# 86 more products on TensorE behind the last one of an attention, expert and MLP kernel

## The chip, the cores and the metric

The kernel runs on one core of a Trainium2 chip. The metric is the device time of one execution in microseconds, and all times here are microseconds unless marked ns. The engines are TensorE (PE; its loads of weights are listed as PEld), VectorE (DVE), ScalarE (ACT), GpSimd (POOL) and SyncE (SP), which issues most of the transfers.

## The reference

Three layers stand one behind the other, over 2304 tokens of width 512. Cut to what matters:

```
x = block_causal_attention(q, k, v)           # 4 x 8 heads x 576 x 64, blocks of 64
x = top-2 mixture of 8 experts(x)             # relu(x @ w1[e]) @ w2[e], weighted
h = x @ w_in                                  # 512 -> 2048
g = h * clip(h + 3, 0, 6) / 6
out = g @ w_out                               # 2048 -> 512
```

All in float32. Only the last two lines are at work where the change is made.

## The kernel before

Products are made in float32r. A value that needs more bits is split into a high and a low part (xh, xl; hh, hl; wah, wal; wbh, wbl), and three products make one: high by high, high by low, low by high.

The last layer (L1450 to L1508) works through groups of token tiles, the list GR. A tile has 128 tokens; the last groups have four tiles, 512 tokens. For each group the 2048 hidden columns are walked in 16 steps f of 128, two to a pair of weight tiles. Function m_s1 makes one step of the first product: s1 (L434) runs four parts of the inner dimension with mm3 (L428), so 12 products of 512 columns, into an accumulator named h. That tile comes from the pool ps_h, which has two buffers of one PSUM bank each. ACT and DVE read it (L1454, L1455) and make hh and hl. Function m_s2 makes the step of the second product one pair of weights later: s2 (L1089) runs three products (L1102 to L1104) for each tile into four accumulators y0 to y3, which collect over all 16 steps. With the last step the tiles are done: DVE scales tiles 0 and 2 (L1469), ACT tiles 1 and 3 (L1467), and SP sends each to the output (L1472).

The order on each engine is that in which the code is written here; an instruction waits only for the semaphores of what it reads or overwrites. Behind the last instruction the program's end (recorded under L1536) is run: SP waits for the transfers and for the engines, each engine drains, and all five meet in a barrier.

The tiles xh and xl of the last group, 128 partitions by 4 parts by 512 tokens each, are under `xT["m", len(GR) - 1]`. KD is 4, the parts of the inner dimension.

Of the kernel before, what the change touches and what calls it, by code (L numbers as in the profile page):

```python
# [7 lines left out]
F32 = mybir.dt.float32  # L8
# [144 lines left out]
def kernel(  # L153
# [1126 lines left out]
    def gather(gi, t):  # L1280
        rows = (E - 1) * CAP + EARLY * 128 if gi == 0 else E * CAP + OVF * 128
        ys = []
        for s_, w in info(gi, t):
            a = work.tile([128, DM], F32, tag="xn", name="ga", bufs=XB)
            nc.gpsimd.indirect_dma_start(  # L1285
                out=a, out_offset=None, in_=y_tab[0:rows, :],
                in_offset=bass.IndirectOffsetOnAxis(ap=s_, axis=0),
            )
            ys.append((a, w))
        gath[gi, t] = ys  # L1290
# [187 lines left out]
    for i in range(len(pairs2) + 1):  # L1478
        for r in range(2):
# [27 lines left out]
            if i < len(pairs2) and f % 2 == 0 and f // 2 < nt:  # L1507
                gather(gi + 1, f // 2)  # L1508


_INS = ["q", "k", "v", "moe_w_gate", "moe_w_noise", "moe_noise", "moe_w1", "moe_w2", "moe2_w_in", "moe2_w_out"]
_OUTS = [((2304, 512), "float32")]
# [28 lines left out]
```

## Time and profile before

| | |
|---|---|
| runs | 1084.88, 1082.29, 1084.93 |
| median | 1084.88 |
| profiled execution, its own time | 1082.07 |
| its span, first to last instruction | 1080.2 |
| granted TensorE clock, mean over the span | 0.998 of full |

The span is inside the profiled execution's time; 1.87 lie around it. In a row of a product, the time is from its start to its modelled end, and the next product starts before that end: how often TensorE can start one is read from the differences of the starts. A product's form is written as the rows and columns of its stationary operand (128*128), then the output's partitions and columns (128x512).

### The profile page before, as it was taken

The page shows a single profiled execution, that of the slowest core. Times are in us where ns is not written, and L with a number is a line of the kernel's source. Part 1 is how long each engine was busy: PE and PEld are TensorE (multiplying, and loading weights), DVE is VectorE, ACT ScalarE, POOL GpSimd, SP SyncE. Part 2 cuts the span into 40 slices and gives each one's busy share as a digit, 9 for nine tenths or more (in the row PEclk, how much of TensorE's full clock was granted, in tenths as well). Part 3 has the DMA queues.
Part 4 walks back from the last instruction along what each step waited for, and adds up shares of the span by engine and source line. Part 5 has one row for each costly group of instructions (what it writes and reads, how often), then busy time and mean ns, then how long its engine had stood idle before and what let it go on. Part 6 is the DMA issues. An engine that isn't in the chain of part 4 may idle for free. (4 is left out here: it accounts for less than half of the span.)

```text
span 1080.2 us, 17109 instructions
## 1 busy us (share of the span) xinstructions
PE 1062.4 (98%) x6189; PEld 932.8 (86%) x6189; DVE 777.3 (72%) x1471; ACT 525.8 (49%) x1061; POOL 295.7 (27%) x346
## 2 busy tenths in 40 slices
PE   7999999999999999999999999999999999999998
PEld 6999999988988989999888898988888888888886
DVE  9778787887698888897887745776655755665452
ACT  6777777754433342424233335664544545454342
POOL 6568687613110101110100001653401420410000
PEclk9999999999999999999999999999999999999999
DMA  7534432116977768766646315312202111201001
GB/s 192 143 89 128 128 89 57 23 43 213 351 250 261 278 221 295 234 214 196 215 153 218 108 35 193 97 39 59 53 26 69 40 49 40 68 10 39 1 1 39
DMA packets 120428, 133.94 MB, mean 124 GB/s; under 512 B 60693, under 2 KB 81685, under 8 KB 120341
## 3 DMA queue, kind: packets, MB, share of 16 engines
q1 hardware_dynamic: 106917, 103.32, 30.7%
q0 software_dynamic: 6080, 19.93, 6.1%
q10 hardware_dynamic: 7344, 9.57, 2.5%
q8 instruction: 50, 0.82, 0.3%
q14 instruction: 37, 0.30, 0.1%
HBM read 92.94 MB, written 36.70 MB: 120 GB/s over the span
## 5 line engine op out<-in xcount | busy, mean ns | idle before, releaser
L430 PE MATMUL h<-xh,wah 128*128 128x512 f32 (+8 forms) x832 | 275.1, 331 | 1.0 <-ACT xh L401 0.8
L431 PE MATMUL h<-xl,wah 128*128 128x512 f32 (+8 forms) x832 | 271.4, 326 | 0.4 <-DVE xl L406 0.3
L432 PE MATMUL h<-xh,wal 128*128 128x512 f32 (+8 forms) x832 | 271.4, 326 | 0.0
L1102 PE MATMUL y<-wbh,hh 128*128 128x512 f32 (+1 forms) x576 | 226.0, 392 | 2.5 <-issue 2.1
L1103 PE MATMUL y<-wbl,hh 128*128 128x512 f32 (+1 forms) x576 | 225.9, 392 | 0.1
L1104 PE MATMUL y<-wbh,hl 128*128 128x512 f32 (+1 forms) x576 | 225.5, 391 | 0.0
L430 PEld LDWEIGHTS h<-xh,wah 128*128 128x128 f32 x832 | 156.5, 188 | 14.8 <-ACT xh L401 1.0
L431 PEld LDWEIGHTS h<-xl,wah 128*128 128x128 f32 x832 | 156.6, 188 | 14.1 <-DVE xl L406 0.9
L432 PEld LDWEIGHTS h<-xh,wal 128*128 128x128 f32 x832 | 156.4, 188 | 11.4
L1104 PEld LDWEIGHTS y<-wbh,hl 128*128 128x128 f32 (+1 forms) x576 | 107.4, 186 | 25.3 <-DVE hl L457 0.8
L1102 PEld LDWEIGHTS y<-wbh,hh 128*128 128x128 f32 (+1 forms) x576 | 107.5, 187 | 23.6 <-issue 2.6
L1103 PEld LDWEIGHTS y<-wbl,hh 128*128 128x128 f32 (+1 forms) x576 | 107.4, 186 | 21.4 <-POOL wbl L385 0.8
L1455 DVE SCALAR_TENSOR_TENSOR r<-r,h 128x512 f32<-128x512 f32 (+1 forms) x80 | 50.5, 631 | 98.1 <-ACT r L1454 97.9
L453 ACT ACTIVATE hh<-h 128x288 fp32r<-128x288 f32 (+7 forms) x128 | 53.3, 416 | 130.6 <-PE h L432 98.1
L385 DVE TENSOR_TENSOR wal<-wa,wah 128x1024 fp32r<-128x1024 f32 x80 | 106.3, 1329 | 13.7 <-ACT wah L381 12.8
L385 DVE TENSOR_TENSOR wbl<-wb,wbh 128x1024 fp32r<-128x1024 f32 x76 | 102.5, 1348 | 14.7 <-ACT wbh L381 14.6
L1454 ACT ACTIVATE r<-h,three 128x512 f32<-128x512 f32 (+1 forms) x80 | 51.6, 645 | 118.7 <-PE h L432 118.7
L1075 POOL DMA_INDIRECT xn<-x_tok,sids x35 | 37.1, 1061 | 254.8 <-PE xps L398 243.4
L1458 DVE TENSOR_TENSOR hl<-r,hh 128x512 fp32r<-128x512 f32 (+1 forms) x80 | 56.0, 700 | 51.5 <-ACT hh L1457 51.5
L381 ACT CAST wbh<-wb 128x1024 fp32r<-128x1024 f32 x80 | 84.0, 1049 | 12.6 <-PE y L1104 10.5
L769 ACT ACTIVATE P<-sb,nm 128x192 f32<-128x192 f32 (+4 forms) x144 | 74.6, 528 | 29.2 <-DVE nm L763 29.2
L1457 ACT CAST hh<-r 128x512 fp32r<-128x512 f32 (+1 forms) x80 | 46.2, 577 | 86.1 <-DVE r L1455 86.1
(265 smaller groups left out, 1765.4 us busy)
## 6 DMA issues: line engine op xcount, KB each, us to landing
wa<-in_moe_w_dram SPq DMA_DIRECT2D x23, 512.0 KB, 6.2
wb<-in_moe_w_dram SPq DMA_DIRECT2D x23, 512.0 KB, 7.1
y_tab<-yo SPq DMA_DIRECT2D x32, 256.0 KB, 4.1
w<-in_moe_w_in_dram SPq DMA_DIRECT2D x16, 512.0 KB, 6.8
y_tab<-zero SPq DMA_DIRECT2D x8, 1024.0 KB, 8.1
w<-in_moe_w_out_dram SPq DMA_DIRECT2D x16, 512.0 KB, 5.3
x_tok<-x SPq DMA_DIRECT2D x32, 144.0 KB, 2.8
wa<-in_moe_w_dram ACTq DMA_DIRECT2D x9, 512.0 KB, 6.3
```

The costliest lines, as they stand in the source:

```text
L381: nc.scalar.copy(w_s[which, u][0], raws[PS[u]][which])
L385: (nc.gpsimd if e == "POOL" else nc.vector).tensor_tensor(lo, raws[PS[u]][which], hi.bitcast(F32), op=OP.subtract)
L430: nc.tensor.matmul(ps, lhsT=wh, rhs=xh, start=first, stop=False)
L431: nc.tensor.matmul(ps, lhsT=wh, rhs=xl, start=False, stop=False)
L432: nc.tensor.matmul(ps, lhsT=wl, rhs=xh, start=False, stop=last)
L453: nc.scalar.activation(h[0][:, c0:c1], ps[:, :c1 - c0], AF.Relu)
L769: nc.scalar.activation(o, views.pop((p, i)), AF.Exp, bias=nms.pop((p, i)), scale=1.0, accum_out=rs[p % 3][:, i:i + 1])
L1102: nc.tensor.matmul(yps[t][:n], lhsT=hh[:, sl], rhs=wh[:, f % 2], start=first, stop=False)
L1103: nc.tensor.matmul(yps[t][:n], lhsT=hh[:, sl], rhs=wl[:, f % 2], start=False, stop=False)
L1104: nc.tensor.matmul(yps[t][:n], lhsT=hl[:, sl], rhs=wh[:, f % 2], start=False, stop=last)
L1454: nc.scalar.activation(r[:, :n], ps[:, :n], AF.Relu, bias=three, scale=1.0)
L1458: nc.vector.tensor_tensor(hl[:, :n], r[:, :n], hh[:, :n].bitcast(F32), op=OP.subtract)
```

## The change

Behind the last loop, 86 products are written. Each has a part of xl as its stationary operand and the same part of xh as its moving operand; all start and end their accumulation in one instruction, and nobody reads the two accumulators pa and pb, which are taken from ps_h under the same tag as h. A product named full uses 128 rows of the array; low uses partitions 0 to 63 and writes pa, high uses partitions 64 to 127 and writes pb. The stationary operand has 128 columns in all of them.

```
+    xh, xl = xT["m", len(GR) - 1]
+    pa, pb = (ps_h.tile([128, 512], F32, tag="h", name="h") for _ in range(2))
+
+    def trial(n, rows, ps, k):
+        nc.tensor.matmul(ps[:, :n], lhsT=xl[rows, k % KD, 0:128], rhs=xh[rows, k % KD, :n], start=True, stop=True)
+
+    full, low, high = slice(0, 128), slice(0, 64), slice(64, 128)
+    for k in range(8):
+        trial(512, full, (pa, pb)[k % 2], k)
+    for n in (512, 384, 288, 256, 128):
+        for k in range(6):
+            trial(n, low, pa, k)
+            trial(n, high, pb, k)
+    for k in range(4):
+        trial(512, full, (pa, pb)[k % 2], k)
+        trial(512, low, pa, k)
+        trial(512, high, pb, k)
+    for k in range(6):
+        trial(256, low, pa, k)
```

So there are 8 full products of 512 columns, 6 pairs at each of five widths, 4 rounds of one full product and a pair of 512 columns, and 6 products of 256 columns on the lower half alone. The last product raises TensorE's semaphore, for which SP waits among its closing waits.

On TensorE the rows behind the last product of the fourth tile (y_11015 is the accumulator of that tile) are these, with + for what is new:

```order
 L1103 MATMUL y_11015<-wbl,hh 128x512
 L1104 MATMUL y_11015<-wbh,hl 128x512
-L1536 UNCONDITIONAL_BRANCH
+L1514 MATMUL h<-xh,xl 128x512 x20
+L1514 MATMUL h<-xh,xl 128x384 x12
+L1514 MATMUL h<-xh,xl 128x288 x12
+L1514 MATMUL h<-xh,xl 128x256 x12
+L1514 MATMUL h<-xh,xl 128x128 x12
+L1514 MATMUL h<-xh,xl 128x512 x12
+L1514 MATMUL h<-xh,xl 128x256 x6
+L1556 UNCONDITIONAL_BRANCH
```

Seven runs of products stand between the last old one and the branch to the program's end; the first 20 are the 8 full ones and the 6 pairs of 512 columns. No other engine's rows move; the branch has only another line number.

## Rows read from the trace of the kernel before

**Rows 1.** The page: busy time by engine, slices of TensorE's clock, the closing chain.
```profile
PE 1062.4 (98%) x6189; PEld 932.8 (86%) x6189; DVE 777.3 (72%) x1471; ACT 525.8 (49%) x1061; POOL 295.7 (27%) x346
...
PEclk9999999999999999999999999999999999999999
...
PE 34%; POOL 1%; DVE 1%; ACT 1%; issue 0%
```

**Rows 2.** Timeline of the end: start, length, engine, line, form, idle time before and its releaser.
```profile
1068.66 0.69 DVE L1455 SCALAR_TENSOR_TENSOR r<-r,h 128x512 f32<-128x512 f32 x1 [3.46 <-ACT r L1454]
...
1074.27 0.39 PE L1104 MATMUL y<-wbh,hl 128*128 128x512 f32 x1
...
1075.63 0.39 PE L1104 MATMUL y<-wbh,hl 128*128 128x512 f32 x1
1076.06 0.60 ACT L1467 ACTIVATE yo<-y 128x512 f32<-128x512 f32 x1 [0.76 <-PE y L1104]
1076.10 0.91 SPq L1472 DMA_DIRECT2D out_dram<-yo  x2
```

**Rows 3.** Output transfers (L1472) and program's end (L1536): ns min/median/max, first and last start.
```profile
DMA to landing us min/median/max: 2.0/2.1/2.1
...
L1536 SPq EVENT_SEMAPHORE  x9: 28/28/28, 1077.1 to 1079.1; - x9
...
L1536 SPq EVENT_SEMAPHORE  x11: 17/28/28, 1077.1 to 1080.2; - x11
...
L1536 PEldq DRAIN  x2: 13/2140/4267, 1071.8 to 1079.6; - x2
```

**Rows 4.** Last stretch: length; PE, PEld, DVE, ACT, POOL busy; granted clock; DMA share; GB/s.
```profile
1077.00:1081.00 4.00, 0.00 (x0) 0.00 (x0) 0.00 (x0) 0.00 (x0) 0.00 (x0) 0.66 0.34 130
```

**Rows 5.** Timeline of TensorE: first and last product of rows of 384, 288 and 256 columns.
```profile
612.77 0.34 PE L430 MATMUL h<-xh,wah 128*128 128x384 f32 x1
...
614.17 0.34 PE L432 MATMUL h<-xh,wal 128*128 128x384 f32 x1
...
367.62 0.30 PE L430 MATMUL h<-xh,wah 128*128 128x288 f32 x1
...
369.08 0.30 PE L432 MATMUL h<-xh,wal 128*128 128x288 f32 x1
...
235.00 0.28 PE L430 MATMUL h<-xh,wah 128*128 128x256 f32 x1
...
235.94 0.28 PE L432 MATMUL h<-xh,wal 128*128 128x256 f32 x1
```

**Rows 6.** Timeline of TensorE in the attention: narrow products, and stationary operands of 64 columns.
```profile
22.89 0.60 PE L781 MATMUL tb<-ident,P 128*128 128x128 f32 x4
...
33.68 0.28 PE L755 MATMUL sb<-kh,qd0h 128*128 128x64 f32 x1
...
33.90 0.28 PE L755 MATMUL sb<-kh,qd0l 128*128 128x64 f32 x1
...
27.52 0.25 PE L813 MATMUL tb<-pth,sp_v 128*128 128x192 f32 x1
27.61 0.28 PE L813 MATMUL tb<-ptl,sp_v 128*64 128x192 f32 x2
27.73 0.50 PE L813 MATMUL tb<-pth,sp_v 128*128 128x64 f32 x2
```

**Rows 7.** Groups of weight loads by form: busy us, mean ns of one, idle before.
```profile
L813 PEld LDWEIGHTS tb<-ptl,sp_v 128*64 128x64 f32 x96 | 11.6, 136 | 0.0
...
L1104 PEld LDWEIGHTS y<-wbh,hl 128*128 128x128 f32 x544 | 102.2, 188 | 23.2 <-DVE hl L457 0.8
```

**Rows 8.** Two stretches near the start, in the columns of rows 4.
```profile
10.00:15.00 5.00, 2.63 (x16) 1.85 (x16) 4.48 (x10) 3.15 (x9) 3.28 (x4) 1.00 0.39 71
15.00:20.00 5.00, 4.15 (x18) 3.74 (x18) 4.81 (x10) 3.32 (x8) 4.09 (x6) 0.68 0.63 134
```

## The prediction

> **What bounds the kernel now.** I read the page first, then the last microseconds as a timeline, then the program's closing rows. TensorE (PE) is busy 98% of the span at a granted clock of 9 tenths or more in all 40 slices, and the closing chain is a row of its products [rows 1]. The last three groups of instructions before the end step from product to product without a gap: L1104 starts at 1074.27 and, six products later, at 1075.63, so a product of 512 columns takes 1.36/6 = 0.227 [rows 2]. The last product starts at 1075.63 and lasts 0.39, to 1076.02. ScalarE scales that tile from 1076.06 for 0.60, and SyncE issues its last output transfer, two issues taking from 1076.10 to 1077.01 [rows 2]. A transfer lands 2.1 after its issue [rows 3], so the last one, issued at about 1076.7, lands at about 1078.8. SyncE runs through its closing waits from 1077.1 to 1079.1; 1.1 later, at 1080.2, the last barrier event ends the span [rows 3]. TensorE had reported itself drained at 1071.8 + 4.27 = 1076.07 [rows 3], and from 1077 on no engine computes at all, while the DMA engines still move the outputs [rows 4]. So TensorE bounds the kernel up to 1076.0 and the landing of the last output bounds it behind that. What is hung behind the last product has about three microseconds in which it costs nothing, from 1076.0 to 1079.0; after that each microsecond counts in full, because the barrier waits for TensorE too.
>
> **The change, part by part.** Nothing is removed or moved. 86 products are added behind the last one on TensorE, and they wait for nothing: the two accumulators come from the pool of the h tiles, whose last reader (VectorE, L1455) runs from 1068.66 for 0.69 and is done at 1069.35 [rows 2], and the operands are the last group's token tiles, in use since long before. Nobody waits for their results, so ACT, VectorE and the output transfers at 1076 to 1079 go on as before. The first added product therefore starts one step behind the last old one, at 1075.63 + 0.227 = 1075.86.
>
> What one product costs is its step, from its start to the next start, not the 0.39 of its row, since products overlap. Steps by width, all with a stationary operand of 128 columns that is loaded for each product: 512 columns 0.227 [rows 2]; 384 columns 612.77 to 614.17 in eight steps, 0.175 [rows 5]; 288 columns 367.62 to 369.08 in eleven, 0.133 [rows 5]; 256 columns 235.00 to 235.94 in eight, 0.118 [rows 5]. Below that the step stops falling: four products of 128 columns take 0.60 in all, and with 0.28 for the last one, as a product of 64 columns has it, the three steps are 0.107; products of 64 columns start at 33.68 and, two further, at 33.90, 0.11 apart [rows 6]. I take 0.109. That floor is the loading of the weights, and not the product: with a stationary operand of only 64 columns the step falls to 0.09 and 0.03, from 27.52 to 27.61 and on to 27.73 [rows 6], and the load itself is shorter, 0.136 against 0.188 [rows 7]. So: a full load occupies the loading path for 0.109, and a product occupies its part of the array for its columns.
>
> No row of this trace has a product on half of the array's rows: the stationary operand is written rows*columns, and it is 128*128 or 128*64 everywhere [rows 6, 7]. So what a pair costs has to be bounded. The upper end is one behind the other: each of a pair pays its own step. The lower end is a pair that costs what one product costs. A middle value follows from the load: the two halves stream side by side, but the two loads still come one after the other, so a pair takes the larger of one product's step and 2 x 0.109 = 0.218. That is 0.227 for 512 columns and 0.218 for 384, 288, 256 and 128.
>
> The three sums. The 8 full products take 8 x 0.227 = 1.82, and the last six, all on the lower half, 6 x 0.118 = 0.71, in every case.
> - One behind the other: five widths, 12 products each, 12 x (0.227 + 0.175 + 0.133 + 0.118 + 0.109 = 0.762) = 9.14; the four rounds of one full and two halves 12 x 0.227 = 2.72. Sum 14.39.
> - Middle: 6 x (0.227 + 4 x 0.218 = 1.099) = 6.59; four rounds 8 x 0.227 = 1.82. Sum 10.94.
> - Lower end: 6 x 0.762 = 4.57; four rounds 1.82. Sum 8.92.
>
> I take the middle. The halves have rows, weights and accumulators of their own, which speaks for products side by side. For the loads the nearest row is the floor at 64 and 128 columns: loads of 0.188 overlap in part and still come no closer than 0.109 to each other [rows 6, 7], and a load of 64 rows has as many columns as one of 128. Both ends stay in the range.
>
> In the sentences of the Trainium skill: TensorE: Matmul & The Clock Gate, LDWEIGHTS (loading the stationary operand), says that a load's time goes with the columns and not with the rows, which speaks for the middle; the estimate by that section, 128/1.2 = 107 ns, agrees with the floor of 109 above. Part 3 of that page (Packing small matmuls) has products on different row groups start some 4 ns apart, which would give the lower end where loads don't hold them up. No run here shows either for half rows yet.
>
> From the sum to the time. The last product of 256 columns starts at 1075.86 + 10.94 - 0.12 = 1086.68 and lasts 0.28 [rows 5], so TensorE ends at 1086.96. Behind it stands the closing sequence of SyncE and the barrier, which took 1.1 from the last of SyncE's waits and 1.4 from the last landing [rows 3]; I take 1.2. Span 1088.2 in place of 1080.2: 8.0 more. That is 10.94 + 0.16 (the last product's own length less its step) + 1.2, less the 4.34 that already lay between 1075.86 and the end. The profiled execution took 1082.07 with 1.87 around its span, so the changed one would take 1090.0 on that footing. The runs of before lie at two levels, 1082.07 and 1082.29, and 1084.88 and 1084.93; the median is of the upper one, 2.8 above the profiled execution. I can't say which level a median of the changed kernel falls on, so I add the 8.0 to the middle, 1083.5: **1091.5**.
>
> **The rivals.**
> *One behind the other.* Nothing in the trace shows two products started together; the shortest step is 0.03, between narrow ones [rows 6]. Then 14.39 replaces 10.94: 11.4 more than before, 1093.5 on the profiled footing and 1096.3 on the upper one.
> *Loads side by side too.* The loads of two halves go to different rows, and already overlap in part. Then 8.92: 5.9 more, 1088.0 on the profiled footing, 1089.4 on the middle.
> *Switching costs a drain.* The change goes between full and half products 9 times (once ahead of the pairs, then eight times in the rounds). If the array had to run empty each time, a switch would cost 0.39 - 0.227 = 0.16, and with the next load (0.188) uncovered 0.35: 1.5 to 3.2 on top, 1093.0 to 1094.7 on the middle. Against it: the trace goes from a stationary operand of 128 columns to one of 64 and back at steps of 0.09 and 0.03, while those products last 0.25 and more [rows 6], so no drain there. TensorEngine Tiling of the Trainium skill, Key Properties, states that changing the tiling mode drains TensorE; the column change in those rows disagrees, a row change is not shown.
> *The clock falls.* From 10 to 15 PE was busy only 2.63 of 5, and from 15 to 20 the granted clock was 0.68 of full, the lower level for most of that stretch [rows 8]. If a stretch of half-array products had the same effect and the clock were at 1.2 GHz for the second half of the 9.1 behind the full products, they would take 4.6 more: 1096.1 on the middle. Against it: TensorE stays busy without a gap.
> *Not slower: the unread products are left out.* Nothing reads them. If the step that turns the program into instructions dropped them, or all but those that fit into the 3.0 of cover (13 at 0.227), the time would be that of before, 1083.5 on the middle. The point is 3.0: it decides from the moment that TensorE's end passes 1079.0. Against it: the built program holds all seven rows, and even the lower end is 8.92.
>
> **How the numbers follow.** Middle 0.36, loads side by side 0.28, one behind the other 0.22, drain 0.05, clock 0.05, left out 0.04. The range is the lower end on the profiled footing to one behind the other on the upper level, 1087.5 to 1096.5; outside are left-out products, part of the clock case, and one behind the other with drains. A difference of 0.3%, 3.3 microseconds, is about what a measurement of this kernel can tell from no change. All cases but the last add at least 5.9; only the lower end, if its median fell on the lower level, could come within 3.3. So faster 0.01, same 0.06, slower 0.93.
>
> **What would show it.** The profile of the changed kernel needs a group of the added line with 86 products, the first at about 1075.86 and no idle time ahead of it. The starts decide between the three: in the 128-column pairs, low to low is 0.22 by the middle, 0.11 by the lower end and 0.22 by the upper, so the 512-column pairs have to tell the rest: 0.23 against 0.45. In the four rounds a step longer than 0.23 ahead of each change shows a drain. The granted clock of 1078 to 1086 shows the fall. The closing sequence is right if the last product's end lies about 1.2 ahead of the span's end. Rows under 86, or a span of 1080, make the forecast wrong altogether.

## The result and the profile after

| | before | changed |
|---|---|---|
| runs | 1084.88, 1082.29, 1084.93 | 1091.49, 1092.03, 1090.79 |
| median | 1084.88 | 1091.49 |
| profiled execution, its own time | 1082.07 | 1091.49 |
| its span | 1080.2 | 1089.7 |

The ratio of the runs is 1.0068, with a 95% interval from 1.0044 to 1.0093: 6.6 microseconds slower by the medians, 4.8 to 10.1 by the interval. The forecast was 1091.5.

The two profiled executions differ by 9.5 in span, and that is not all due to the change. What the change touches begins with the last old product, so I measure from its start to the end of the span: 4.62 before (1075.63 to 1080.25), 12.31 after (1077.39 to 1089.70). The change added **7.69**; the forecast's sum had 7.96. The other 1.77 arose ahead of any added instruction.

The page of the changed kernel, with what answers to [rows 1]:

```profile
span 1089.7 us, 17282 instructions
...
PE 1072.6 (98%) x6275; PEld 938.9 (86%) x6275; DVE 776.6 (71%) x1471; ACT 526.2 (48%) x1061; POOL 296.7 (27%) x346
...
PEclk9999999999999999999999999999999999999999
...
PE 35%; POOL 1%; DVE 1%; ACT 1%; issue 0%
PE y L1103 6%; PE y L1104 6%; PE y L1102 6%; PE h L432 6%; PE h L430 6%; PE h L431 6%; PE h L1514 1%; POOL ga L1285 1%; DVE wal L385 0%; POOL ga L1297 0%; POOL wbl L385 0%; ACT wah L381 0%; DVE r L1455 0%; DVE hl L1458 0%; ACT hh L1457 0%
```

86 more products (6275 for 6189), with 10.2 more busy time on TensorE and 6.1 more on its loads; the other engines have as many instructions as before. The line of the added products is now in the closing chain. The timeline of TensorE and of its weight loads in the same stretch (start, length, form, count) answers to [rows 2]:

```profile
1077.39 0.40 PE L1104 MATMUL y<-wbh,hl 128*128 128x512 f32 x1
1077.63 10.89 PE L1514 MATMUL h<-xh,xl 128*128 128x512 f32 x86
...
1077.40 1.78 PEld L1514 LDWEIGHTS h<-xh,xl 128*128 128x128 f32 x8
1079.53 4.96 PEld L1514 LDWEIGHTS h<-xh,xl 64*128 64x128 f32 x61 [0.35 <-issue]
1084.73 0.19 PEld L1514 LDWEIGHTS h<-xh,xl 64*128 64x128 f32 x2 [0.24 <-issue]
1085.16 0.19 PEld L1514 LDWEIGHTS h<-xh,xl 128*128 128x128 f32 x1 [0.24 <-issue]
1085.59 0.19 PEld L1514 LDWEIGHTS h<-xh,xl 64*128 64x128 f32 x2 [0.24 <-issue]
```

Three things are to be seen. The first added product starts at 1077.63, 0.23 behind the last old one, so there is no wait. Two loads of a pair take 0.19 together (1084.73, x2), the time of one: the loads of two halves go side by side. And in the rounds, loads start 0.43 apart (1084.73, 1085.16, 1085.59) with the loading path idle for 0.24 ahead of each, where an undisturbed product of 512 columns has a step of 0.227: each change of rows costs 0.2.

The groups of the added line by form (busy time, mean ns of one, idle time before) show no idle time ahead of the products. A load of 64 rows lasts as long as one of 128 rows:

```profile
L1514 PEld LDWEIGHTS h<-xh,xl 64*128 64x128 f32 x74 | 5.9, 185 | 1.6 <-issue 1.3
...
L1514 PEld LDWEIGHTS h<-xh,xl 128*128 128x128 f32 x12 | 2.2, 187 | 1.1 <-issue 0.7
L1514 PE MATMUL h<-xh,xl 64*128 64x256 f32 x18 | 1.7, 278 | 0.0
L1514 PE MATMUL h<-xh,xl 64*128 64x384 f32 x12 | 1.2, 336 | 0.0
...
L1514 PE MATMUL h<-xh,xl 64*128 64x288 f32 x12 | 0.9, 290 | 0.0
...
L1514 PE MATMUL h<-xh,xl 64*128 64x128 f32 x12 | 0.8, 263 | 0.0
```

The starts of single products, read from the trace, give the steps. Inside a pair, high starts 3 to 4 ns behind low at every width. From pair to pair:

| columns | 512 | 384 | 288 | 256 | 128 |
|---|---|---|---|---|---|
| step of a pair | 0.234 | 0.177 | 0.131 | 0.118 | 0.112 |
| step of one full product, before | 0.227 | 0.175 | 0.133 | 0.118 | 0.109 |

(Medians from low to low; the two steps at the first change, 0.318 and 0.335, and the 0.06 at the first pair of 128 columns are left out.) A pair costs what one product costs, at every width, within 7 ns.

The end of the program, in the columns of [rows 3]:

```profile
L1556 SPq EVENT_SEMAPHORE  x12: 17/28/7727, 1078.8 to 1089.6; - x12
...
L1556 PEldq DRAIN  x2: 13/1699/3385, 1085.2 to 1089.0; - x2
```

SyncE waited 7.7 in one closing wait, for TensorE, and TensorE's drain ended at 1085.2 + 3.39 = 1088.6. The last product ended at 1088.52 and the span at 1089.70, 1.18 later. The stretches in the columns of [rows 4] show the clock:

```profile
1077.60:1079.50 1.90, 1.90 (x9) 1.32 (x7) 0.23 (x1) 0.60 (x1) 0.00 (x0) 1.00 1.00 380
1079.50:1084.30 4.80, 4.80 (x61) 4.44 (x60) 0.00 (x0) 0.00 (x0) 0.00 (x0) 1.00 0.12 47
1084.30:1087.30 3.00, 3.00 (x12) 1.30 (x10) 0.00 (x0) 0.00 (x0) 0.00 (x0) 1.00 0.00 0
1087.30:1088.50 1.20, 1.20 (x9) 0.95 (x8) 0.00 (x0) 0.00 (x0) 0.00 (x0) 1.00 0.00 0
```

It was full throughout. The four stretches are the full products, the pairs, the rounds and the six single halves.

### The profile page after: what moved, and what is told of

Same layout as the page of the kernel before. It is cut to its first block, busy times and chain, and to the rows that moved or that the text cites. A ratio compares the mean times of both kernels' runs of the same rounds, so it can differ in the third digit from the quotient of the medians.

```text
span 1089.7 us, 17282 instructions
## 1 busy us (share of the span) xinstructions
PE 1072.6 (98%) x6275; PEld 938.9 (86%) x6275; DVE 776.6 (71%) x1471; ACT 526.2 (48%) x1061; POOL 296.7 (27%) x346
## 5 line engine op out<-in xcount | busy, mean ns | idle before, releaser
L430 PE MATMUL h<-xh,wah 128*128 128x512 f32 (+8 forms) x832 | 275.0, 330 | 1.3 <-ACT xh L401 0.8
L430 PEld LDWEIGHTS h<-xh,wah 128*128 128x128 f32 x832 | 156.4, 188 | 15.4 <-DVE hl L457 1.3
```

The lines of the kernel that those rows point to most:

```text
L430: nc.tensor.matmul(ps, lhsT=wh, rhs=xh, start=first, stop=False)
```

## The experiments

My theory after the two traces: pairs are free (products and loads side by side), each change between full and half rows costs 0.2, and the first three microseconds are covered. All edits are shown against the changed kernel, in or behind its helper `trial`. All but the first are single executions, each with its own trace. The measure is the time from the start of the last old product to the end of the span; a single execution's total time varies by some microseconds ahead of that start, which the measure leaves out.

**Only twelve full products.**

```
+    for k in range(12):
+        trial(512, full, (pa, pb)[k % 2], k)
```

(in place of all loops.)

> Only 12 full products of 512 columns stand behind the last one; the 74 others are left out. The measure in all these runs is the time from the start of the last old product to the end of the span: 4.62 before, 12.31 in the changed kernel. If the cover behind the last product is what the forecast says (about 3.0), 12 products end 0.227 + 12 x 0.227 + 0.16 = 3.11 behind that start, while SyncE's last wait stands 3.5 behind it, so the measure stays at 4.6 to 4.7 and the time is that of before. Rival: TensorE's work at the end costs from its first product on, because the barrier or the transfers are held up by it; then the measure grows by up to 2.7, to 7.3.

Measured: 1084.62 against 1084.34 of before in the same job, ratio 1.0, interval 0.9991 to 1.001. The measure is 4.61, from 1079.49 to 1084.1:

```profile
1079.49 0.40 PE L1104 MATMUL y<-wbh,hl 128*128 128x512 f32 x1
1079.50 2.69 PEld L1514 LDWEIGHTS h<-xh,xl 128*128 128x128 f32 x12
1079.73 2.89 PE L1514 MATMUL h<-xh,xl 128*128 128x512 f32 x12
1079.93 0.60 ACT L1467 ACTIVATE yo<-y 128x512 f32<-128x512 f32 x1 [0.77 <-PE y L1104]
```

2.89 of products end at 1082.62, 1.5 ahead of the end, and cost nothing. The cover is as the forecast had it, and these twelve products disturb neither the transfers nor the barrier.

**The same 86 products, sorted by rows.**

```
-    for k in range(8):
+    for k in range(12):
         trial(512, full, (pa, pb)[k % 2], k)
     for n in (512, 384, 288, 256, 128):
-        for k in range(6):
+        for k in range(10 if n == 512 else 6):
             trial(n, low, pa, k)
             trial(n, high, pb, k)
-    for k in range(4):
-        trial(512, full, (pa, pb)[k % 2], k)
-        trial(512, low, pa, k)
-        trial(512, high, pb, k)
```

> The same 86 products, sorted: 12 full ones first, then the 34 pairs, then the 6 single halves, so that the rows change once and not 9 times. If each change between full and half rows costs the 0.2 that the rounds showed (0.425 for a step in place of 0.227), 8 of them go and the measure falls by 1.65, from 12.31 to 10.7. If the rounds are slow for another reason that lies in their 12 products themselves (the 512 columns on two halves at the end of the program), nothing falls: 12.3.

Measured: 10.77, that is 1.53 less than 12.31 with the same products; 10.7 was expected. The loads now run without the idle times of the rounds:

```profile
1078.16 2.69 PEld L1514 LDWEIGHTS h<-xh,xl 128*128 128x128 f32 x12
1081.20 6.33 PEld L1514 LDWEIGHTS h<-xh,xl 64*128 64x128 f32 x74 [0.35 <-issue]
```

One idle time is left, at the one change. Eight changes cost 1.53 together, 0.19 each. In this run the high product falls behind the low one, by up to 37 ns, and the pairs cost no more for it: the two halves needn't march in step.

**Without the high halves.**

```
             trial(n, low, pa, k)
-            trial(n, high, pb, k)
...
         trial(512, low, pa, k)
-        trial(512, high, pb, k)
```

> All 34 products on the high half are left out; the rest stands as in the changed kernel. If both products and both loads of a pair go side by side, the high ones cost nothing and the measure stays at 12.3 (within 0.1). If the loads of a pair come one after the other at 0.109, as the forecast had it, single products are shorter than pairs: 6 x (0.043 + 0.085 + 0.100 + 0.109) = 2.0 less, 10.3. The rounds also tell a change of rows from a repeated accumulator: full and low use the same one only in every other round, so by the accumulator only two of the four rounds pay 0.2, by the rows all four do.

Measured: 13.95, longer than with the 34 products that are left out. The two parts have to be read apart. The five widths, from the first half product to the first full one of the rounds, took 4.77 with 30 products and 4.78 with 60 in the changed kernel: the high ones cost nothing, and loads in series (2.0 less) are refuted. In the rounds the first four steps are 0.424, 0.430, 0.431 and 0.431, so all rounds pay, whichever accumulator the full product used: it is the rows. Then the steps rise to 0.60 and 0.72, and the last singles take 0.214 in place of 0.118. That I had not expected. The granted clock tells why:

```profile
1080.20:1085.00 4.80, 4.80 (x31) 4.41 (x30) 0.00 (x0) 0.00 (x0) 0.00 (x0) 1.00 0.13 50
1085.00:1087.00 2.00, 2.00 (x6) 0.92 (x5) 0.00 (x0) 0.00 (x0) 0.00 (x0) 0.98 0.00 0
1087.00:1089.00 2.00, 2.00 (x4) 0.77 (x4) 0.00 (x0) 0.00 (x0) 0.00 (x0) 0.50 0.00 0
1089.00:1091.00 2.00, 1.88 (x7) 1.48 (x7) 0.00 (x0) 0.00 (x0) 0.00 (x0) 0.50 0.00 0
```

About 2 into the rounds the clock fell to half, 1.2 GHz, though PE reads as busy until its last product.

**Both of a pair on the same half.**

```
-            trial(n, high, pb, k)
+            trial(n, low, pb, k)
...
-        trial(512, high, pb, k)
+        trial(512, low, pb, k)
```

> The high half's products are moved to the low half (same accumulator as before), so both of a pair use the same rows. If the pairs are cheap because two halves work at once, this costs the second product in full: 6 x 0.762 + 4 x 0.227 = 5.5 more, 17.8. If they are cheap because a product of 64 rows takes half of the time, it costs nothing: 12.3.

Measured: 21.24. The five widths took 9.37, 4.59 more than as pairs on two halves (6 x 0.762 = 4.57 expected): a product of 64 rows costs as much as a full one, and it is the two halves at once that make it free. The rest is again the clock. It held through nine microseconds of single half products and fell about 0.5 into the rounds, which start at 1088.01:

```profile
1079.00:1083.00 4.00, 4.00 (x21) 3.48 (x20) 0.00 (x0) 0.00 (x0) 0.00 (x0) 1.00 0.05 20
1083.00:1087.00 4.00, 4.00 (x33) 4.00 (x32) 0.00 (x0) 0.00 (x0) 0.00 (x0) 1.00 0.00 0
1087.00:1088.50 1.50, 1.50 (x12) 1.18 (x11) 0.00 (x0) 0.00 (x0) 0.00 (x0) 1.00 0.00 0
1088.50:1090.00 1.50, 1.50 (x4) 0.70 (x3) 0.00 (x0) 0.00 (x0) 0.00 (x0) 0.50 0.00 0
```

**Rounds at three widths.** What is a change of rows made of?

```
+    for n in (512, 256, 128):
+        for k in range(8):
+            trial(n, full, (pa, pb)[k % 2], k)
+            trial(n, low, pa, k)
+            trial(n, high, pb, k)
```

(in place of all that follows the 8 full products.)

> 8 full products, then 8 rounds of one full product and a pair at each of three widths: 512, 256 and 128 columns; 80 products, 48 changes of rows. Three theories of the change: (a) the array runs empty and the next load lies in the open, so a step is the load's 0.107, the columns' own time and about 0.1: 0.43, 0.32 and 0.27 for the three widths, rounds of 0.85, 0.64 and 0.53, the measure 19.7; (b) a fixed 0.2 on top of the usual step: 0.43, 0.32 and 0.31, rounds of 0.86, 0.64 and 0.62, the measure 20.3; (c) a fixed step of 0.425 whatever the width: 23.8.

Measured: 22.77. The total lies near theory (c), but the steps refute it: while the clock was full, 0.43 at 512 columns and 0.31 at 256, as (a) and (b) both have it. Timeline of the loads, with a step of 0.43 between neighbours, and then at a later one of 0.51:

```profile
1085.26 0.19 PEld L1514 LDWEIGHTS h<-xh,xl 128*128 128x128 f32 x1 [0.25 <-issue]
1085.69 0.19 PEld L1514 LDWEIGHTS h<-xh,xl 64*128 64x128 f32 x2 [0.25 <-issue]
1086.13 0.19 PEld L1514 LDWEIGHTS h<-xh,xl 128*128 128x128 f32 x1 [0.25 <-issue]
...
1091.15 0.29 PEld L1514 LDWEIGHTS h<-xh,xl 128*128 128x128 f32 x1 [0.23 <-issue]
1091.66 0.29 PEld L1514 LDWEIGHTS h<-xh,xl 64*128 64x128 f32 x2 [0.22 <-issue]
```

In the rounds of 256 columns the granted clock fell (1.00 from 1088 to 1090, 0.54 from 1090 to 1092), after 6.8 of rounds of 512 columns that had left it full, and all rounds of 128 columns ran at half, at 0.40 a step:

```profile
1088.00:1090.00 2.00, 2.00 (x12) 1.24 (x11) 0.00 (x0) 0.00 (x0) 0.00 (x0) 1.00 0.00 0
1090.00:1092.00 2.00, 2.00 (x8) 1.15 (x7) 0.00 (x0) 0.00 (x0) 0.00 (x0) 0.54 0.00 0
```

So the total is theory (a) or (b) with the clock on top, and this run doesn't tell the two apart, because they differ at 128 columns.

**The same rounds with 64 columns in the stationary operand.**

```
-    def trial(n, rows, ps, k):
-        nc.tensor.matmul(ps[:, :n], lhsT=xl[rows, k % KD, 0:128], rhs=xh[rows, k % KD, :n], start=True, stop=True)
+    def trial(n, rows, ps, k, m=128, o=0):
+        nc.tensor.matmul(ps[o:o + m, :n], lhsT=xl[rows, k % KD, o:o + m], rhs=xh[rows, k % KD, :n], start=True, stop=True)
...
+            trial(n, full, (pa, pb)[k % 2], k, 64)
+            trial(n, low, pa, k, 64)
+            trial(n, high, pb, k, 64)
```

> As the rounds of three widths, but in these rounds the stationary operand has 64 columns in place of 128, which shortens its load (0.136 against 0.188 in the profile of before, and a floor of 0.055 against 0.109). If the load lies in the open at a change of rows, each step gets some 0.05 shorter at all three widths: 0.37, 0.27 and 0.21, the measure about 17.0. If the change costs a fixed 0.2 that has nothing to do with the load, 512 and 256 columns stay at 0.43 and 0.32: about 19.4.

Measured: 17.58. At the full clock the steps are 0.38, 0.26 and 0.20 for the three widths, 0.05 shorter at 512 and 256 columns than with the load of 128 columns:

```profile
1085.05 0.13 PEld L1514 LDWEIGHTS h<-xh,xl 64*64 64x64 f32 x2 [0.25 <-issue]
1085.43 0.13 PEld L1514 LDWEIGHTS h<-xh,xl 128*64 128x64 f32 x1 [0.25 <-issue]
1085.81 0.13 PEld L1514 LDWEIGHTS h<-xh,xl 64*64 64x64 f32 x2 [0.25 <-issue]
```

The load takes 0.13 in place of 0.19 and the whole saving reaches the step; the idle time ahead of it, 0.25, stays. So theory (a) is right in its main point: at a change of rows the next load waits until the running product is through, and lies in the open. The clock fell here too, in the middle of the rounds of 128 columns, which is why the measure passes 17.0.

What a change is made of follows from differences of steps. A column takes 0.42 ns by the steps of full products (0.227 at 512 and 0.133 at 288 columns), so 512 columns take 0.215 and 256 take 0.107. Taking these off the steps of the two runs (0.43 and 0.31; 0.38 and 0.26), some 0.21 remain with the load of 128 columns and 0.16 with that of 64. The 0.05 between them are 64 columns of load; twice that is the whole load, 0.107 by [rows 6], and 0.1 is left. That this rest is the array running empty, as theory (a) has it, is not shown. At half the clock the columns and the load take twice as long, but the rest does not. A step of 512 columns was 0.72 (in the run without the high halves) and one of 256 was 0.51, so 256 columns take 0.21; a step of 128 columns was 0.40 with the long load and 0.30 with the short one, so the long load takes 0.21; and 0.51 - 0.21 - 0.21 leaves 0.09.

**Change of columns.**

```
+            trial(n, full, (pa, pb)[k % 2], k)
+            trial(n, full, pa, k, 64)
+            trial(n, full, pb, k, 64)
```

(in the rounds, with the helper of the run above.)

> The rounds of three widths, but with all 128 rows throughout: one product with a stationary operand of 128 columns, then two with one of 64 columns. So the columns change and the rows don't. By the steps of 0.09 and 0.03 in the attention of the kernel before, a change of columns costs nothing: rounds of 0.68, 0.34 and 0.22, the measure 13.3. If a change of columns empties the array as a change of rows does, 48 changes cost 0.2 each: about 22.9. The Trainium skill, TensorEngine Tiling, Key Properties, has every change of the tiling mode drain TensorE and would have the second.

Measured: 13.48; no change cost anything. The loads run on with no idle time at 80 products and 47 changes (24 to the short operand, 23 back; the 48 expected is one too many):

```profile
1076.82 12.14 PEld L1514 LDWEIGHTS h<-xh,xl 128*128 128x128 f32 x80
```

The statement of TensorEngine Tiling (Trainium skill, Key Properties), that a change of the tiling mode drains TensorE, fits the rows here: a change costs about 0.2, though no run shows that draining is what takes it. A stationary operand of 64 columns in place of 128 costs nothing; whether such a product changes the tiling mode in that sense, no run shows.

**Four quarters.**

```
+    px = ps_x.tile([128, 512], F32, tag="x", name="h")
+    py = ps_y.tile([128, 512], F32, tag="y0", name="h")
...
+    for n in (512, 384, 288, 256, 128):
+        for k in range(6):
+            for r, ps in enumerate((pa, pb, px, py)):
+                trial(n, slice(32 * r, 32 * r + 32), ps, k)
```

(in place of the pairs and the rounds.)

> 8 full products, then at each of the five widths 6 sets of four products of 32 rows, one on each quarter of the rows and each into an accumulator of its own, then 6 single halves of 256 columns; 134 products. If four quarters work at once as two halves do, a set costs one step of its width: 6 x 0.762 = 4.6, and with two changes of rows the measure is about 9.1. If only two go at once, it is about 13.7; one after the other, 22.8.

Measured: 9.09, as expected for four at once. 134 products run from 1076.14 to 1083.81; the 30 sets of four took 4.79, as long as 30 pairs:

```profile
1076.14 7.67 PE L1514 MATMUL h<-xh,xl 128*128 128x512 f32 x134
```

**Long stretches of pairs, and of single halves.** Two runs for the clock:

```
+    for k in range(60):
+        trial(512, low, pa, k)
+        trial(512, high, pb, k)
```

(in place of all that follows the 8 full products.)

> 8 full products, then 60 pairs of 512 columns and nothing else, one change of rows. Pairs at 0.23 with no gap: 1.82 + 0.19 for the change + 60 x 0.23 = 15.8, and 1.57 around it: the measure 17.4, the granted clock full throughout. If a long stretch of pairs brings the clock down as the long stretches of rounds did, steps of 0.45 appear and the measure passes 20.

> 8 full products, then 60 products of 512 columns on the low half alone. In the runs where the clock fell (low halves alone, the pairs moved to one half, the rounds of three widths) it fell during rounds, so two causes are left: half of the rows being empty, or the time that the array stands still at each change of rows. If the empty rows do it, the clock falls here too: steps go from 0.23 to 0.43 and the measure to 22 or more. If it is the standing still, the steps stay at 0.23 and the measure is 17.4, as with pairs.

The second run has the same loop without the high half. Measured: 17.26 and 17.25. The timeline and two stretches of each, pairs and then singles:

```profile
1078.35 15.82 PE L1514 MATMUL h<-xh,xl 128*128 128x512 f32 x128
...
1080.00:1085.00 5.00, 5.00 (x44) 3.91 (x44) 0.00 (x0) 0.00 (x0) 0.00 (x0) 1.00 0.17 64
1085.00:1090.00 5.00, 5.00 (x48) 4.13 (x46) 0.00 (x0) 0.00 (x0) 0.00 (x0) 1.00 0.01 3
```

```profile
1077.93 15.82 PE L1514 MATMUL h<-xh,xl 128*128 128x512 f32 x68
...
1080.00:1085.00 5.00, 5.00 (x23) 4.01 (x24) 0.00 (x0) 0.00 (x0) 0.00 (x0) 1.00 0.08 31
1085.00:1090.00 5.00, 5.00 (x24) 4.06 (x23) 0.00 (x0) 0.00 (x0) 0.00 (x0) 1.00 0.00 0
```

60 more products, to the hundredth no more time. The clock stayed full in both, so half-empty rows alone, at 512 columns, don't bring it down. What does stays open. In all four runs in which it fell, it fell during rounds, but the time lost at the changes doesn't explain that by itself: 6.8 of rounds of 512 columns left the clock full in the run of three widths, and 3.3 of them did in the changed kernel. In the run on one half it fell after only 0.5 of rounds, behind narrow half products, and in the runs of three widths only in the rounds of 256 or 128 columns. The expectation of the last run named two causes; the narrow half products are a third, and no run tries a long stretch of them alone.

## Why the prediction was right, and where it was not

The value came out within 0.01 of the median. That close a hit is luck: two terms were wrong by about as much in opposite directions (1.81 too much for the pairs, 1.52 too little for the rounds), and the footing of 1083.5, a guess between two levels, lies 1.4 under the median of before, while the 7.96 of the sum lies 1.35 over the difference of the medians, so that these cancel too.

| term | forecast | measured |
|---|---|---|
| 8 full products | 1.82 | 1.91 |
| pairs at five widths | 6.59 | 4.78 |
| four rounds | 1.82 | 3.34 |
| six single halves | 0.71 | 0.71 |
| sum of the steps | 10.94 | 10.74 |
| last product's end to the end of the span | 1.2 | 1.18 |
| added behind the last old product | 7.96 | 7.69 |

(The 7.96 takes the old end as 1080.2; with 1080.25 it is 7.91. Measured terms are differences of starts: 1077.63, 1079.54, 1084.31, 1087.65, and 1088.24 + 0.12. The 1.91 holds part of the first change.)

- *The bound and the cover* were right: TensorE's end now decides, and the first three microseconds are free. Twelve full products alone left the time unchanged.
- *No wait ahead of the first product* was right: 0.23 behind the last old one.
- *The step of a full product*, 0.227 [rows 2], and of the narrow ones [rows 5, 6] were right, and hold for a pair as a whole.
- *The choice of the middle for pairs was wrong.* It let the two loads of a pair follow one another at 0.109. The rows it rested on [rows 6, 7] show loads to the same rows of the array; they say nothing on loads to different halves. Those go side by side. The rival "loads side by side too" was right here, 1.8 less. Of the two statements of the Trainium skill that I had set against each other (TensorE: Matmul & The Clock Gate, LDWEIGHTS and Part 3, Packing small matmuls), both agree with the trace: a load of 64 rows takes 185 ns where one of 128 rows takes 187, and products on two row groups start 3 to 4 ns apart. What I had concluded from the first, that the loads of a pair queue, is not in it.
- *The cost of a change of rows was wrong at nothing.* The rival "switching costs a drain" was right with its price: 0.16 with the load covered, 0.35 with the load's full 0.188 in the open; measured 0.19 to 0.2, where 0.107 of load and 0.1 of a rest not explained lie in the open, in place of what the usual step holds besides the columns. Its argument against, the change of columns in [rows 6], was a true row of the wrong kind: the run with changing columns has no cost either, and the rows do. Nine changes make about 1.7. (The trace of before has stationary operands of 80, 88 and 112 columns too, not only of 128 and 64; all have 128 rows, which is what the argument needed.)
- The two rivals together give 8.92 + 9 x 0.19 = 10.6, against 10.74 measured. I gave them as alternatives; they are two independent questions, and the forecast should have crossed them.
- *The clock* did not fall in the changed kernel (1.00 in all four stretches), but the rival is real: in four of the experiments it did. A stretch of half products alone, as I had it, was not enough at 512 columns (60 of them left it at 1.00); which part of the rounds, or of the narrow products ahead of them, brought it down is open.
- *The footing.* The 1.77 that the changed kernel's execution was late before the change began is scatter: the start of the last old product lies between 1075.6 (before) and 1079.5 (the run with twelve full products, whose time is that of before) in the 12 profiled executions of this case, all with the same program up to there. In the changed kernel's trace the first products of the expert stage start as early as before (228.6 against 228.7); it is late by 0.6 halfway through L430's products and by 1.8 at three quarters of them. What makes it so was not followed further. The two levels are not there either: of the 13 runs of before beside the first experiment (1082.65 to 1085.77), 8 lie between 1082.29 and 1084.88.
- The 6.61 between the medians, the 7.69 of the traces and the 7.96 of the sum all lie in the interval of 4.8 to 10.1.

## What to carry to other kernels

Products on separate halves or quarters of the array's rows, each into an accumulator bank of its own, run at the price of one, loads included; but each change between full and partial rows costs about 0.2 here, so sort them into long stretches. Work hung behind the last product is free up to the landing of the last output, and in full after that. When two unknown mechanisms can both be true, forecast their four combinations and not two stories, and look whether the row that argues against one is of the same kind.

## What the hardware showed that I had not expected

- Two loads of 128 columns to different halves take 0.19 together; four quarters' products and loads still take one step (30 sets in 4.79).
- At a change of rows the next load lies in the open, 0.107 for 128 columns and half of that for 64, with 0.1 besides that half the clock left at 0.09; a change of the stationary operand's columns between 128 and 64 costs nothing (13.48 with 47 changes).
- The granted clock fell to half while PE read as busy for 2.00 of 2.00, in rounds of full and half products: at steps of 0.43 in the two runs whose half products went to one half only, at 0.31 and 0.20 in the two with rounds of three widths. Pairs in rounds of 512 columns (6.8 long) and 60 gapless half products left it at 1.00. The cause is open.
